# Windowed attention and a gated MLP on one core: 168 keys per 64 queries, four-step scores, split weighing sums, and a new order of all engines

## The chip, the core and the metric

The kernel runs on one core of a Trainium2 chip. The metric is device time in microseconds (us) of one launch, lower is better; runs of the same kernel are compared by their median. A change of less than 0.2% (1.2 us here) can't be told from no change.

Names of the engines, as the profile has them: PE is TensorE's matmuls and PEld its weight loads, DVE is VectorE, ACT ScalarE, POOL GpSimd, SP SyncE, which here only issues DMAs.

## The reference

```python
batch, n_heads, seq, head_dim = (4, 8, 768, 64)
n_global, n_local = (8, 96)

scores = scale * np.matmul(q, k.transpose(0, 1, 3, 2))
keep = (pos[None, :] < n_global) | ((rel >= 0) & (rel < n_local))     # rel = query - key
scores = np.where(keep, scores - slopes * dist, -1e9)
a = np.exp(scores - scores.max(-1, keepdims=True))
a = a / (a.sum(-1, keepdims=True) + 1e-9)
x = np.matmul(a, v)                      # to (3072 tokens, 512)

h = x @ w_in                             # 512 x 2048
g = h * np.tanh(np.log1p(np.exp(h)))
out = g @ w_out                          # 2048 x 512
```

Each query sees the 96 keys up to itself and the first 8 keys of its sequence. All inputs are float32. The kernel computes most products in float16 as three: a number is cut into a high and a low half, and high x high, high x low and low x high are summed in PSUM.

## The kernel before, in words

The 3072 tokens are 12 chunks of 256 (`ci` = 0 to 11; three chunks are one sequence). A chunk has two blocks of 128 queries (`blk`), and attention goes by steps `t`: eight to a chunk, `t = 8*ci + 4*g + 2*blk + a2`, each for one block and one pair of heads. The first block of a sequence sees only its own 128 keys, every other block sees 232: the 96 before it, the 8 global ones, and its own 128. The first three chunks (`CF32`) do attention in float32 with PE transposes. From `ci` = 3 on (the fourth chunk) it is float16 in halves, and these are its steps, with the letters by which the program calls them:

- `s` **scores**: one call does two steps (`a2` = 0, 1), 24 matmuls of 64 rows x 64 columns x 168 moving elements: three products, two heads (upper and lower half of the array), and two halves of 64 queries (`need`, left and right half of the array). Output is in two PSUM banks, `SC`.
- `t` **largest** (DVE): adds the bias mask `mb` and takes the maximum over 232 columns. `y` **exps** (ACT): exponential and sum of the row.
- `g`, `p` **high_a, low_a**: the two float16 halves of the weights, 512 numbers per partition each (232 padded to two blocks of 128, two heads).
- `X` **turn_a**: a DMA transpose of 8 blocks of 128, issued by SP, gives `AT`.
- `W` **weigh**: for each head, 6 matmuls: three products for the 104 far keys (`vc`) and three for the 128 own keys (`vo`). Stationary is `AT`, 128 columns wide; 64 elements move. 12 matmuls a step, 6 in a first block.
- `x` **window_v**: copies the far rows of v to partitions 0 to 103 of `vc`, two DMAs per block. `R`, `T`, `U`, `V` divide by the row sums, cut in halves and turn the result into `xT`.

The MLP of a chunk is eight blocks `m`: `i` **moe_in** (24 matmuls of 256 elements), `j u n r G H z Z` on ACT, DVE and POOL, and `o` **moe_out** (12 matmuls of 512 elements). `Q` and `Y` bring the output out. `k` are checks at the end: a matmul of ones counts bad values (`k1`), and DVE reduces the count to one flag (`k2`), which every engine reads before the program may end.

The weights come as float64 words, and are made into float16 halves by DVE, ACT and POOL (`w A S B C D E`) during about the first 160 us. `e` are matmuls on a constant tile that do nothing but occupy PE.

The order of the whole work is a list written into the program, `PROGRAM`: each engine and each queue takes its own instructions in the order of this list, and never another. Letter and number are the step and its index; a `'` sends a copy or a subtraction to DVE instead of ACT or POOL.

```python
need = [(slice(0, D), slice(0, WN - D)), (slice(D, P), slice(D, WN))]           # scores, not a first block
for kk in range(nk):                                                            # weigh
    for x, y in ((0, 0), (0, 1), (1, 0)):
        nc.tensor.matmul(pav[:, cols], AT[rows_, (x * 2 + j) * nk + kk, :], vs[kk][rows_, y, cols], ...)
```

Of the kernel before, what the change touches and what calls it, by code (L numbers as in the profile page):

```python
# [110 lines left out]
def windowed(st, tc, loc):  # L111
# [14 lines left out]
    OWN = FB  # L126
    STEP = P + NGMAX
# [101 lines left out]
    def window_v(ci):  # L229
        b, c = divmod(ci, NCHB)  # L230
        vc = stk.tile([P, 2, DM], F32, name="vc")
        if ci < CF32:
            far = L.v[b, 0:NGMAX, :]
# [55 lines left out]
    mb0 = cp.tile([P, H, P], BF16, name="mb0")  # L289

# [9 lines left out]
    def units(i):  # L300

        for m in (mb0, mb):
            nc.vector.tensor_scalar(m, m, SQ, None, op0=ALU.mult)

    fills = []

    def begin(n):  # L310

        if not fills:
            fills.append(mt.tile([P, DM], I32, name="ws", bufs=WB).bitcast(F16)[:, 0:DM])
            nc.vector.memset(fills[0], 1.0)
        fill = fills[0]
        bank = ps.tile([P, 2, CH], F32, name="ph").rearrange("p j t -> p (j t)")
        for i in range(n):
            nc.tensor.matmul(bank, fill[:, 0:P], fill, start=True, stop=True)
# [87 lines left out]
    def width(nk):  # L406
        return P if nk == 1 else WN

    def blocks(A, nk):
        if nk == 1:  # L410
            return A[:, :, 0:P].unsqueeze(2)
        return bass.AP(A.tensor, A.offset, [list(A.ap[0]), [W, 2], [FB, 2], [1, P]])

# [4 lines left out]
    def scores(t):  # L418

        ci, g, blk, _, first, nk = shape(t)  # L420
        w = width(nk)
        sc = SC
        col0 = OWN if first else blk * STEP
        rows_ = slice(blk * P, (blk + 1) * P)
        if ci < CF32:
            qr, kr = raw[2 * ci + g]
            terms = ((qr, kr),)
        else:
            (qh, ql), (kh, kl) = split[2 * ci + g, "q"], split[2 * ci + g, "k"]
            terms = ((qh, kh), (ql, kh), (qh, kl))  # L430
        need = [(slice(0, D), slice(0, D)), (slice(D, P), slice(0, P))] if first else [(slice(0, D), slice(0, WN - D)), (slice(D, P), slice(D, WN))]
        for a2 in range(2):
            for n, (x, y) in enumerate(terms):
                for j in range(2):
                    half = slice(j * D, (j + 1) * D)
                    for r, c in need:
                        nc.tensor.matmul(sc[j][r, a2, c], x[half, a2, blk * P + r.start:blk * P + r.stop], y[half, a2, col0 + c.start:col0 + c.stop], start=(n == 0), stop=(n == len(terms) - 1))  # L437
            pend[t + a2] = [x[:, a2] for x in sc]

    def largest(t):  # L440
        ci, g, blk, a2, first, nk = shape(t)
        w = width(nk)
# [5 lines left out]
        for j in range(2):  # L448
            h = g * GH + 2 * a2 + j
            m = mb0[:, h, :] if first else mb[:, h, :]  # L450
# [3 lines left out]
    def exps(t):  # L454
        ci, g, blk, a2, first, nk = shape(t)
        rs, nm = stat[ci, blk]
        A = pend[t][:, :, 0:width(nk)]
# [4 lines left out]
    def halved(t):  # L462
        nk = shape(t)[-1]
        A, hl = pend[t]
        flat = hl.rearrange("p a b w -> p (a b w)")[:, 0:4 * nk * P]
        return blocks(A, nk), flat, flat.rearrange("p (a b k w) -> p a b k w", a=2, b=2, k=nk), nk

    def high_a(t, other=False):
        pend[t] = (pend[t], at.tile([P, 2, 2, W], F16, name="hl", bufs=3))
        A, _, hl, _ = halved(t)  # L470
        copy(hl[:, 0], A, 1.0, other)

    def low_a(t, other=False):
        A, _, hl, _ = halved(t)
        rest(hl[:, 1], A, hl[:, 0], other)

    def turn_a(t):
        _, flat, _, nk = halved(t)
        AT = at.tile([P, 8, P], F16, name="AT", bufs=4)
        nc.sync.dma_start_transpose(AT[:, 0:4 * nk, :], flat)  # L480
# [18 lines left out]
    def weigh(t):  # L499
# [5 lines left out]
        vs = [vown[ci][:, blk]] if nk == 1 else [vcmp[ci][:, blk], vown[ci][:, blk]]  # L505
        if ci < CF32:
            pair = slice((g * GH // 2 + a2) * P, (g * GH // 2 + a2 + 1) * P)
# [5 lines left out]
            return  # L513
        for j in range(2):
            h = g * GH + 2 * a2 + j
            cols = slice(h * D, (h + 1) * D)
            n, last = 0, 3 * nk - 1
            for kk in range(nk):
                rows_ = slice(0, P if kk == nk - 1 else FB)
                for x, y in ((0, 0), (0, 1), (1, 0)):  # L520
                    nc.tensor.matmul(pav[:, cols], AT[rows_, (x * 2 + j) * nk + kk, :], vs[kk][rows_, y, cols], start=(n == 0), stop=(n == last))  # L521
                    n += 1
# [23 lines left out]
    def times_rb(n, other=False):  # L546
# [3 lines left out]
        rbs = at.tile([P, DM], F32, name="rb", bufs=1)  # L550
# [155 lines left out]
    v1 = cp.tile([1, NALL], F32, name="v1")  # L706
# [4 lines left out]
    def checks(i):  # L711
# [36 lines left out]
        e8 I0 x0 q1 v0 K0 K1 M0' M3' L3' L0 L1 L5 M2 L2 s0 e4 t0 t1 f0 M5' y0 L6 M1 y1 L4 s2 P1 P0 t3 F1' y3 t2 w0 q2 e2 P3 q3 x1 w2 v1 F3' L7' y2 F0 s4 W1  # L748
        P2 W0 t5 t4 M7' F2' M4' y5 y4 M6 B0 R0 s6 P4 W3 P5 O0 t6 A0' t7 S0' F4 w1 y6 F5 y7 P6 s8 C0 t8 P7 W5 W4 W2 t9 m0 R1 D0 F6 y8 F7 w3 q4 s10 P8 T0' t10
        t11 B2 A2' U0 y9 O1 P9 s12 W7 W6 w7 w4 w5 x2 q5 v2 w6 t13 y10 m1 F9 F8 y11 P10 W9 P11 W8 t12 S2' F11' B1 T1' C2 y13 F10 y12 E0 s14 W10 P12 W11 P13  # L750
# [213 lines left out]
```

## Time and profile before

| what | us |
|---|---|
| median of 3 runs | 606.42 (605.76 to 606.97) |
| the profiled execution, its own time | 605.27 |
| its span, first to last instruction | 603.4 |
| PE busy, share of the span | 594.3, 98% |
| ACT / DVE / POOL busy | 454.1 / 437.1 / 150.7 |

The first three lines of time differ by what lies around the span (1.87 us) and by the spread of the runs. Busy time is the union of an engine's instructions; since matmuls are pipelined, the time that a matmul costs is better read from one start to the next than from its duration. PE's clock was granted in full over the whole span, but for the first few microseconds.

### The profile page before, as it was taken

The numbers are of one execution on the slowest core, as the hardware profiler recorded it, in microseconds if no ns is written. First come the engines' busy times: TensorE is split into PE (matmuls) and PEld (weight loads), VectorE is DVE, ScalarE is ACT, GpSimd is POOL, SyncE is SP. The second block draws the span as 40 slices with busy tenths as digits, with TensorE's granted clock in tenths as the row PEclk, the third lists the DMA queues.
The fourth block names the chain that finished last, engine by engine and source line by source line (L and its number), as shares of the span: only waits on it lengthen the run. The fifth ranks groups of instructions, "written<-read, shape, count | busy, mean of one in ns | idle before, by whom it ended". The sixth has DMA issues, their size and how long they took to land.

```text
span 603.4 us, 15002 instructions
## 1 busy us (share of the span) xinstructions
PE 594.3 (98%) x5775; PEld 412.3 (68%) x5775; DVE 437.1 (72%) x1188; ACT 454.1 (75%) x1130; POOL 150.7 (25%) x128
## 2 busy tenths in 40 slices
PE   7999999999999999999999999999999999999997
PEld 3678677785567676767666676767667766766784
DVE  7899988998978795693876667675786777462433
ACT  6899999989978777569766778677877864665653
POOL 0033321331040423123134422141242121301020
PEclk9999999999999999999999999999999999999999
DMA  8999664332295481634354443562446241310001
GB/s 207 275 261 337 230 167 132 107 97 64 80 197 110 64 213 32 166 98 113 66 147 113 134 122 92 146 147 55 106 62 150 68 111 44 89 36 0 36 1 39
DMA packets 123387, 71.14 MB, mean 118 GB/s; under 512 B 91792, under 2 KB 113168, under 8 KB 123312
## 3 DMA queue, kind: packets, MB, share of 16 engines
q1 hardware_dynamic: 122736, 69.88, 46.3%
q8 instruction: 46, 0.75, 0.5%
q10 hardware_dynamic: 576, 0.27, 0.3%
q14 instruction: 29, 0.24, 0.1%
HBM read 38.62 MB, written 6.29 MB: 74 GB/s over the span
## 4 chain that ended last, share of the span: by engine, by line
PE 90%; DMA 5%; ACT 2%; SPq 1%; issue 0%; DVE 0%; ACTq 0%; DVEq 0%
PE ph L597 41%; PE po L662 36%; PE pav L662 4%; PE pav L521 4%; PE sc L437 4%; DMA kr<-kd 2%; DMA AT<-hl 2%; DMA vo<-v 2%; PE pav L512 1%; PE ph L490 1%; SPq L480 0%; PE ph L543 0%; ACT A L460 0%; ACT u L623 0%; ACT AT L148 0%
## 5 line engine op out<-in xcount | busy, mean ns | idle before, releaser
L597 PE MATMUL ph<-xT,wts 128*128 128x256 f16 x2304 | 263.5, 273 | 0.0
L597 PEld LDWEIGHTS <-wts 128*128 128x128 f16 x2304 | 223.1, 98 | 34.5 <-issue 0.4
L662 PE MATMUL po<-wts,gt 128*128 128x512 f16 (+1 forms) x1056 | 234.5, 374 | 0.0
L662 PEld LDWEIGHTS <-gt 128*128 128x128 f16 x1248 | 115.7, 98 | 118.1
L615 ACT ACTIVATE e<-ph 128x512 f32<-128x512 f32 x90 | 53.2, 591 | 96.3 <-PE ph L597 96.1
L152 POOL TENSOR_TENSOR gt<-gf,gt 128x512 f16<-128x512 f32 x50 | 61.9, 1240 | 228.8 <-DVE gt L146 154.5
L635 DVE CUSTOM_DVE_ANT_0 gf<-gf,u 128x512 f32<-128x512 f32 x96 | 72.4, 757 | 49.5 <-ACT u L627 47.6
L460 ACT ACTIVATE A<-A,nm 128x232 f32<-128x232 f32 (+1 forms) x192 | 88.2, 461 | 11.9 <-DVE nm L451 11.9
L631 DVE SCALAR_TENSOR_TENSOR gf<-e,ph 128x512 f32<-128x512 f32 x90 | 61.0, 683 | 49.3 <-ACT e L615 48.3
L152 POOL TENSOR_TENSOR hl<-A,hl 128x512 f16<-128x512 f32 (+1 forms) x43 | 50.3, 1179 | 110.6 <-ACT hl L148 43.5
L451 DVE CUSTOM_DVE_ANT_0 A<-sc,mb 128x232 f32<-128x232 f32 (+1 forms) x192 | 63.6, 375 | 12.8 <-PE sc L437 12.7
L627 ACT ACTIVATE u<-u 128x512 f32<-128x512 f32 x96 | 59.7, 625 | 1.9
L619 ACT ACTIVATE u<-e 128x512 f32<-128x512 f32 x96 | 59.8, 624 | 1.7
L623 ACT ACTIVATE u<-u 128x512 f32<-128x512 f32 x96 | 59.7, 623 | 1.6
L152 POOL TENSOR_TENSOR wts<-ws,wts 128x512 f16<-128x512 f32 x18 | 22.7, 1267 | 82.3 <-ACT wts L148 75.6
L152 DVE TENSOR_TENSOR gt<-gf,gt 128x512 f16<-128x512 f32 x46 | 34.3, 748 | 6.9 <-ACT gt L148 6.3
L460 ACT ACTIVATION_READ_ACCUMULATOR A<-A,nm 128x1 f32 x192 | 36.2, 188 | 0.0
L521 PEld LDWEIGHTS <-AT 128*128 128x128 f16 (+1 forms) x792 | 29.3, 97 | 7.6 <-DMA AT<-hl 1.2
L148 ACT ACTIVATE gt<-gf 128x512 f16<-128x512 f32 x39 | 24.3, 623 | 11.3 <-DVE gmax L635 9.2
L662 PE MATMUL pav<-wts,gt 128*128 128x512 f16 (+1 forms) x192 | 28.7, 299 | 0.0
L521 PE MATMUL pav<-vo,AT 128*128 128x64 f16 x432 | 28.0, 192 | 0.0
L146 DVE TENSOR_SCALAR gt<-gf 128x512 f16<-128x512 f32 x57 | 25.7, 453 | 1.5
(130 smaller groups left out, 563.3 us busy)
## 6 DMA issues: line engine op xcount, KB each, us to landing
wts<-w_in SPq DMA_DIRECT2D x12, 512.0 KB
wts<-w_out SPq DMA_DIRECT2D x12, 512.0 KB
qr<-qT SPq DMA_DIRECT2D x23, 256.0 KB
kr<-kd SPq DMA_DIRECT2D x32, 184.0 KB
out<-ob SPq DMA_DIRECT2D x23, 256.0 KB
vr<-v SPq DMA_DIRECT2D x9, 512.0 KB
vc<-vo SPq DMA_DIRECT2D x15, 192.0 KB
wr<-w_in SPq DMA_DIRECT2D x4, 512.0 KB
```

Source lines behind the costliest of these rows:

```text
L152: (nc.vector if other else nc.gpsimd).tensor_tensor(out, in_, high, op=ALU.subtract)
L451: nc.vector.tensor_tensor_reduce(out=A[:, j, 0:w], in0=sc[j][:, 0:w], in1=m, scale=-1.0 / (UNIT if ci < CF32 else UNIT * SQ), scalar=3.0e3 ...
L460: nc.scalar.activation(A[:, j], A[:, j], AF.Exp, bias=nm[:, h:h + 1], scale=-1.0, accum_out=rs[:, h:h + 1])
L521: nc.tensor.matmul(pav[:, cols], AT[rows_, (x * 2 + j) * nk + kk, :], vs[kk][rows_, y, cols], start=(n == 0), stop=(n == last))
L597: nc.tensor.matmul(ph[:, j, :].rearrange("p (b t) -> p b t", b=2), wv4[:, 2 * fb, x, c * P:(c + 1) * P], xT[:, :, y * NCC + c, :], start=( ...
L615: nc.scalar.activation(mish[m]["e"], mish[m]["h"], AF.Exp, scale=-1.0 / (SV * SW), accum_out=esum[:, m:m + 1])
L619: nc.scalar.activation(u, mish[m]["e"], AF.Square, bias=0.5)
L623: nc.scalar.activation(mish[m]["r"], mish[m]["u"], AF.Ln, bias=0.25 / RS, scale=1.0 / RS)
L627: nc.scalar.activation(r, r, AF.Exp, scale=-1.0)
L631: nc.vector.scalar_tensor_tensor(gf, mish[m]["e"], 0.5, mish[m]["h"], op0=ALU.add, op1=ALU.mult)
L635: nc.vector.tensor_tensor_reduce(out=gf, in0=gf, in1=mish[m]["r"], scale=SG / (SV * SW * RS), scalar=0.0, op0=ALU.mult, op1=ALU.max, accum ...
L662: nc.tensor.matmul(pos[ci][t + k][:, cols], gt[:, x, j, t * P:(t + 1) * P], wv4[:, 2 * fb + 1, y, cols], start=(fb == 0 and n == 0), stop= ...
```

## The change

Only chunks from `ci` = 3 on compute otherwise than before:

- Keys are kept per half of 64 queries. A row holds the 168 keys that its half can see (`SEEN` = 104 + 64) instead of 232, so `t` and `y` go over 168 columns and there is a mask `mb2` for it, put together from `mb` by `units`. A first block keeps 128.
- `s` does four steps in one call (two calls a chunk instead of four); only `ci` = 3 keeps two. The second block's scores go to the two `pav` banks, which were for the sums of `W` alone.
- The halves of the weights are 128 columns `main` (key 40 to 167 of the 168) and a block `few`, in which the first 40 keys stand three times side by side: high, low and, for the third product, high again. A transpose has 6 blocks instead of 8.
- `W` does each head as 4 products for each half of 64 queries: three of 128 keys and one of 3 x 40 = 120 rows. That is 16 matmuls a step (12 in a first block) with 64 stationary columns, the two halves side by side in the array; they write to the upper and the lower 64 partitions of `pav`.
- For this `window_v` lays v out anew: per block three larger copies and six of 40 rows, 9 DMAs instead of 2, some of which read what the ones before them have written. For even chunks they go to the buffers `wr` of the weights, which are free by then. Half of the `AT` tiles go to the buffers `hs`.
- `e` uses the broadcast tile of ones (no tile has to be filled first); its calls are 9, 4 and 2 matmuls (before 8, 4, 2). `rb` goes to the buffer of `xhl`, and `v1` to that of `mb`.
- `PROGRAM` is new in all.

```diff
@@ window_v @@
+            src = vo[:, 0] if t else vown[ci - 1][:, 1]
+            far = vo[0:NGMAX, 0] if c == 0 else vcmp[ci - 1][1][P - D - NGMAX:P - D, 0:2]
+            k = P - NPREV + REST
+            nc.sync.dma_start(vb[0:P - k, 0:2], src[k:P])
+            nc.sync.dma_start(vb[P - k:P - D, 0:2], far)
+            nc.sync.dma_start(vb[P - D:P, 0:2], vo[0:D, t])
+            for n, y in enumerate((0, 0, 1)):
+                r = n * REST
+                nc.sync.dma_start(vb[r:r + REST, 2], src[k - REST:k, y])
+                nc.sync.dma_start(vb[r:r + REST, 3], vb[P - D - REST:P - D, y])
@@ scores @@
+            n = 2 if ci == CF32 else 4
+            other = [ps.tile([P, DM], F32, name=f"pav{j}", bufs=1).rearrange("p (a w) -> p a w", a=2) for j in range(2)] if n == 4 else SC
+            for u in range(t, t + n):
+                _, _, blk, a2, first, _ = shape(u)
+                sc = pend[u] = [x[:, a2] for x in (other if blk else SC)]
+                w = width(u)
+                for n, (x, y) in enumerate(((qh, kh), (ql, kh), (qh, kl))):
+                    for j in range(2):
+                        half = slice(j * D, (j + 1) * D)
+                        for r in (0, D):
+                            k = OWN if first else blk * STEP + r
+                            nc.tensor.matmul(sc[j][r:r + D, 0:w], x[half, a2, blk * P + r:blk * P + r + D], y[half, a2, k:k + w], start=(n == 0), stop=(n == 2))
@@ high_a @@
-        copy(hl[:, 0], A, 1.0, other)
+        copy(main[:, 0], A, 1.0, other)
+        if few is not None:
...
+            both = bass.AP(few.tensor, few.offset, [list(few.ap[0]), [P, 2], [2 * REST, 2], [1, k]])
+            copy(both, A[:, :, 0:k].unsqueeze(2).broadcast_to([P, 2, 2, k]), 1.0, other)
@@ weigh @@
-            for kk in range(nk):
-                rows_ = slice(0, P if kk == nk - 1 else FB)
-                for x, y in ((0, 0), (0, 1), (1, 0)):
-                    nc.tensor.matmul(pav[:, cols], AT[rows_, (x * 2 + j) * nk + kk, :], vs[kk][rows_, y, cols], start=(n == 0), stop=(n == last))
+            terms = [(P, j, 0), (P, j, 1), (P, 2 + j, 0)] + ([] if nk == 1 else [(3 * REST, 4 + j, 2)])
+            for n, (k, x, y) in enumerate(terms):
+                for r in range(2):
...
+                    nc.tensor.matmul(pav[r * D:(r + 1) * D, cols], AT[0:k, x, r * D:(r + 1) * D], vs, start=(n == 0), stop=(n == len(terms) - 1))
```

A stretch of the list, the calls that PE gets in chunk 4 (`ci` = 4), before and now, all other letters left out:

```
before  s32 W27 i23 W31 o20 W30 o21 s34 o22 i25 i24 s36 i26 o23 s38 i27 W33 o24 o25 W32 i28 o26 s40 W35 W37 W36 W34 o27
now     s32 o21 o22 i24 s36 i25 i26 o23 i28 o24 i27 W36 W33 W39 W34 W35 W38 W37 W32 i30 o25 o26 s40
```

What moved is that the eight `W` of a chunk now stand in one row, behind both score calls; it is the same in the other eight chunks.

Three places in the order of the engines.

PE, the first weighing of chunk 4, before: `AT` is the turned weight tile, `vc` the far and `vo` the own rows of v, and `pav0` the sum.

```order
L597 MATMUL ph_2920<-xT_2624,wts_96 128x256
L521 LDWEIGHTS AT_2787
L521 MATMUL pav0_2958<-vc_2477,AT_2787 128x64
L521 LDWEIGHTS AT_2787
L521 MATMUL pav0_2958<-vc_2477,AT_2787 128x64
L521 LDWEIGHTS AT_2787
L521 MATMUL pav0_2958<-vc_2477,AT_2787 128x64
L521 LDWEIGHTS AT_2787
L521 MATMUL pav0_2958<-vo_1692,AT_2787 128x64
```

And the first weighing of that chunk now (`hs` is a turned weight tile in its new buffer, `wr` the new layout of v):

```order
L630 MATMUL ph_3120<-xT_2626,wts_97 128x256
L555 LDWEIGHTS hs_2973
L555 MATMUL pav0_3147<-wr_2248,hs_2973 64x64
L555 LDWEIGHTS hs_2973
L555 MATMUL pav0_3147<-vo_1707,hs_2973 64x64
L555 LDWEIGHTS hs_2973
L555 MATMUL pav0_3147<-wr_2248,hs_2973 64x64
L555 LDWEIGHTS hs_2973
L555 MATMUL pav0_3147<-vo_1707,hs_2973 64x64
```

Each full-width matmul has become two of 64 stationary columns, one for each half of the queries; 128 of them now follow one another in a chunk.

SP, the copies of v for chunk 5 (lines 248 and 249) between the transposes (L480 of the weights, L580 of `xT`), before:

```order
L480 DMA_TRANSPOSE AT<-hl 128x8x128
L580 DMA_TRANSPOSE xT<-xhl 128x8x128
L248 DMA vc<-vo 96x1024
L249 DMA vc<-vc 8x1024
L248 DMA vc<-vo 96x1024
L249 DMA vc<-vc 8x1024
L480 DMA_TRANSPOSE AT<-hl 128x8x128
```

And now, the first of the two blocks of that chunk (lines 259 to 265), behind the last transpose of chunk 4's weights:

```order
L508 DMA_TRANSPOSE hs<-hl 128x6x128
L259 DMA vc<-vo 56x1024
L260 DMA vc<-wr 8x1024
L261 DMA vc<-vo 64x1024
L264 DMA vc<-vo 40x512
L265 DMA vc<-vc 40x512
L264 DMA vc<-vo 40x512
L265 DMA vc<-vc 40x512
L264 DMA vc<-vo 40x512
L265 DMA vc<-vc 40x512
L259 DMA vc<-vo 56x1024
```

Four DMAs have become eighteen, and both transposes of `xT` now wait behind them.

DVE at the end of the program, before (`v` and `done_i` are the reduction of the checks, `ob` a piece of the output):

```order
L725 TENSOR_SCALAR v_108<-sc_102 1x142
L726 TENSOR_REDUCE v_110<-v_108 1x1
L727 TENSOR_REDUCE v_109<-sc_102 1x12
L728 TENSOR_REDUCE v_110<-v_109 1x1
L729 TENSOR_REDUCE v_110<-sc_102 1x1
L730 TENSOR_TENSOR v_110<-v_110 1x1
L731 TENSOR_SCALAR v_110<-v_110 1x1
L732 SCALAR_TENSOR_TENSOR done_i<-v_110,fl 1x1
L146 TENSOR_SCALAR ob<-pav_8509 128x128
```

And now:

```order
L148 TENSOR_SCALAR ob<-pav_9120 128x128
L758 TENSOR_SCALAR mb<-sc_103 1x142
L759 TENSOR_REDUCE v_110<-mb 1x1
L760 TENSOR_REDUCE v_109<-sc_103 1x12
L761 TENSOR_REDUCE v_110<-v_109 1x1
L762 TENSOR_REDUCE v_110<-sc_103 1x1
L763 TENSOR_TENSOR v_110<-v_110 1x1
L764 TENSOR_SCALAR v_110<-v_110 1x1
L765 SCALAR_TENSOR_TENSOR done_i<-v_110,fl 1x1
```

The reduction has moved behind the last piece of the output, and on PE the matmul that feeds it behind the last `o` (before it stood in front of that).

## Rows read from the trace of the kernel before

**Rows 1.** The page's first part: busy us, share of the span, instructions.

```profile
PE 594.3 (98%) x5775; PEld 412.3 (68%) x5775; DVE 437.1 (72%) x1188; ACT 454.1 (75%) x1130; POOL 150.7 (25%) x128
```

**Rows 2.** Busy time of each engine in five stretches (us from the start).

```profile
core 0: us, PE busy (x) PEld busy (x) DVE busy (x) ACT busy (x) POOL busy (x), PEclk, DMA share, GB/s
0.00:31.20 31.20, 27.20 (x302) 16.80 (x303) 24.80 (x112) 23.38 (x80) 1.95 (x8) 1.00 0.96 241
31.20:60.70 29.50, 29.29 (x350) 22.95 (x348) 28.33 (x95) 28.95 (x80) 10.68 (x9) 1.00 1.03 302
60.70:165.00 104.30, 104.30 (x828) 71.06 (x827) 96.14 (x214) 97.94 (x214) 26.52 (x21) 1.00 0.43 123
165.00:560.00 395.00, 394.53 (x3956) 271.88 (x3954) 270.21 (x723) 283.30 (x716) 105.76 (x87) 1.00 0.45 103
560.00:603.40 43.40, 38.96 (x347) 29.61 (x344) 17.62 (x47) 20.50 (x43) 5.76 (x5) 1.00 0.07 26
```

**Rows 3.** Groups by line and form: busy us, mean ns, idle before.

```profile
L521 PE MATMUL pav<-vo,AT 128*128 128x64 f16 x432 | 28.0, 192 | 0.0
...
L521 PE MATMUL pav<-vc,AT 104*128 104x64 f16 x360 | 24.8, 192 | 0.5 <-DMA AT<-hl 0.4
```

**Rows 4.** Timeline of PE, 300 to 312 us: start, length, instructions merged.

```profile
303.26 2.78 PE L597 MATMUL ph<-xT,wts 128*128 128x256 f16 x24
305.98 0.63 PE L437 MATMUL sc<-wc,ws 64*64 64x168 f16 x24
306.54 2.79 PE L597 MATMUL ph<-xT,wts 128*128 128x256 f16 x24
309.17 0.25 PE L521 MATMUL pav<-vc,AT 104*128 104x64 f16 x3
...
309.80 0.25 PE L521 MATMUL pav<-vo,AT 128*128 128x64 f16 x3
309.88 2.32 PE L662 MATMUL po<-wts,gt 128*128 128x512 f16 x10
```

**Rows 5.** One score call, timeline cut off at 306.06, 306.11 and 306.18 us.

```profile
305.98 0.27 PE L437 MATMUL sc<-wc,ws 64*64 64x168 f16 x4
...
305.98 0.34 PE L437 MATMUL sc<-wc,ws 64*64 64x168 f16 x8
...
305.98 0.41 PE L437 MATMUL sc<-wc,ws 64*64 64x168 f16 x12
```

**Rows 6.** Timeline of PE, 21 to 23.4 us: a float32 step of 64-column matmuls.

```profile
21.10 0.66 PE L490 MATMUL po<-idn,A 128*128 128x128 f32 x4
21.68 1.09 PE L543 MATMUL ph<-idn,ri 128*64 128x128 f32 x16
22.70 0.66 PE L490 MATMUL po<-idn,A 128*128 128x128 f32 x4
```

**Rows 7.** Groups by form: the maxima and the exponentials.

```profile
L460 ACT ACTIVATE A<-A,nm 128x232 f32<-128x232 f32 x160 | 75.8, 476 | 9.8 <-DVE nm L451 9.8
...
L451 DVE CUSTOM_DVE_ANT_0 A<-sc,mb 128x232 f32<-128x232 f32 x160 | 56.0, 392 | 9.6 <-PE sc L437 9.5
...
L460 ACT ACTIVATE A<-A,nm 128x128 f32<-128x128 f32 x32 | 12.4, 388 | 2.0 <-DVE nm L451 2.0
...
L451 DVE CUSTOM_DVE_ANT_0 A<-sc,mb 128x128 f32<-128x128 f32 x32 | 7.6, 286 | 3.2 <-PE sc L437 3.2
```

**Rows 8.** The chain that ended last: two early loads, one wait for a transpose.

```profile
7.74 9.19 DMA kr<-kd
16.94 9.34 DMA vo<-v
...
384.57 4.27 DMA AT<-hl
```

**Rows 9.** Timeline of SP, 300 to 312 us: issues of one transpose and two copies.

```profile
302.32 0.60 SPq L248 DMA_DIRECT2D vc<-vo  x1
...
302.97 0.73 SPq L249 DMA_DIRECT2D vc<-vc  x1
...
305.19 1.27 SPq L480 DMA_TRANSPOSE AT<-hl  x1
```

**Rows 10.** Timeline of the end: the checks on DVE, and PE's last matmuls.

```profile
594.94 0.29 DVE L725 TENSOR_SCALAR v<-sc 1x142 f32<-1x142 f32 x1 [0.96 <-PE sc L722]
...
596.37 0.21 DVE L732 SCALAR_TENSOR_TENSOR done_i<-v,fl 1x1 int32<-1x1 f32 x1
...
598.12 0.83 PE L662 MATMUL pav<-wts,gt 128*128 128x128 f16 x12
```

More of the change, by code (lines that the diff above doesn't have):

```diff
@@ L126, in windowed @@
     OWN = FB
+    SEEN = FB + D
+    REST = SEEN - P
     STEP = P + NGMAX
@@ L298, in mask_far, with units @@
         masked(mb[:, h, :], rel, h, other)
[L300 to L308, printed above, removed]
+    def units(i, other=False):
+        if i == 0:
+            copy(mb0, mb0, SQ, not other)
+        else:
+            half = slice(0, D) if i == 1 else slice(D, P)
+            copy(mb2[half], mb[half, :, 0:SEEN] if i == 1 else mb[half, :, D:], SQ, not other)
     def begin(n):
[L312 to L315, printed above, removed]
         bank = ps.tile([P, 2, CH], F32, name="ph").rearrange("p j t -> p (j t)")
         for i in range(n):
-            nc.tensor.matmul(bank, fill[:, 0:P], fill, start=True, stop=True)
+            nc.tensor.matmul(bank, ones.broadcast_to([P, P]), ones.broadcast_to([P, DM]), start=True, stop=True)
     NPC = 2 * NFB
@@ L404, in shape, with width @@
         return ci, g, blk, a2, first, 1 if first else 2
[L406 to L412, printed above, removed]
+    def width(t):
+        nk = shape(t)[-1]
+        return P if nk == 1 else WN if where(t)[0] < CF32 else SEEN
     SC = [ps.tile([P, 2, W], F32, name=f"sc{j}", bufs=1) for j in range(2)]
@@ L420, in scores @@
         ci, g, blk, _, first, nk = shape(t)
-        w = width(nk)
+        if ci >= CF32:
+            (qh, ql), (kh, kl) = split[2 * ci + g, "q"], split[2 * ci + g, "k"]
+            n = 2 if ci == CF32 else 4
[10 more added lines that the diff above has]
+                            nc.tensor.matmul(sc[j][r:r + D, 0:w], x[half, a2, blk * P + r:blk * P + r + D], y[half, a2, k:k + w], start=(n == 0), stop=(n == 2))
+            return
         sc = SC
         col0 = OWN if first else blk * STEP
[L424 to L430, printed above, removed]
+        qr, kr = raw[2 * ci + g]
         need = [(slice(0, D), slice(0, D)), (slice(D, P), slice(0, P))] if first else [(slice(0, D), slice(0, WN - D)), (slice(D, P), slice(D, WN))]
         for a2 in range(2):
[L433 to L437, printed above, removed]
+            for j in range(2):
+                half = slice(j * D, (j + 1) * D)
+                for r, c in need:
+                    nc.tensor.matmul(sc[j][r, a2, c], qr[half, a2, blk * P + r.start:blk * P + r.stop], kr[half, a2, col0 + c.start:col0 + c.stop], start=True, stop=True)
             pend[t + a2] = [x[:, a2] for x in sc]
@@ L441, in largest @@
         ci, g, blk, a2, first, nk = shape(t)
-        w = width(nk)
+        w = width(t)
         sc = pend[t]
@@ L456, in exps @@
         rs, nm = stat[ci, blk]
-        A = pend[t][:, :, 0:width(nk)]
+        A = pend[t][:, :, 0:width(t)]
         for j in range(2):
```

174 lines of the change are left out of this document (97 added, 77 removed).

## The prediction
> **What bounds the kernel now.** I read the page's busy shares first: PE is at 98%, and no other engine is above 75% [rows 1]. A share over the whole span can hide stages, so the second view is the busy time in five stretches [rows 2]. From 31 to 560 us PE is idle for 0.68 us in all; its idle time lies ahead of that (4.0 us, the first loads) and behind it (4.4 us, the end of the program). DVE and ACT are above 90% until 165 us, while the weights are split, and at 68% and 72% after. So the time is the sum of PE's work, plus a start and an end, as long as the others keep up. An edit is worth what it takes off PE; what it takes off DVE and ACT is worth nothing behind 165 us.
>
> A busy PE says little of what one matmul costs, so I use starts in its timeline. A weighing matmul is listed with 192 ns [rows 3], but 24 of them take from 309.17 to 309.88 us: 0.71 us, 29.6 ns each [rows 4]. A score call takes from 305.98 to 306.54 us, 0.56 us for 24 matmuls [rows 4]. Cut off at three times, it shows 4, 8 and 12 matmuls begun, four more each 0.07 us [rows 5]: the four quarters of the array run side by side, and a set of four costs what 168 elements cost. Six sets are 0.43 us, so 0.13 us of the call is something else. The block ahead of it, 24 matmuls of 256 elements, takes 2.72 us to the score call and 2.63 us where a weighing follows [rows 4]: another 0.1 us. A stay in quarters thus costs 0.23 us beside its work.
>
> **The change, part by part.**
>
> *Scores.* The matmuls and their elements stay: 12 per step, sets of four. (In a first block one of each pair grows from 64 to 128 elements, but its partner was 128 already, so the set's time stays.) Chunks 4 to 11 had four calls and have two: 16 stays fewer, 16 x 0.23 = 3.7 us off PE.
>
> *Weighing sums, before.* 60 steps of 12 and 12 steps of 6 are the 792 matmuls of rows 3; at 29.6 ns, 23.4 us. They come and go without a change of mode.
>
> *Weighing sums, now.* 60 steps of 16 and 12 of 12 are 1104 matmuls of 64 columns, 552 pairs, one of each pair for either half of the array. What a pair costs the trace does not show in float16. Upper bound: one after the other at today's pace, 59 ns. Lower bound: the 64 moving elements alone, by the 0.109 us that 256 elements take [rows 4], 27 ns. The nearest row is the float32 step with 64 columns by 128 rows: 16 matmuls of 128 elements in 1.02 us, 64 ns each, where 4 of the same elements at full width take 0.58 us before it, 145 ns each [rows 6]. Pairs do overlap there. Weight loads of 64 columns keep up with sets of 72 ns [rows 5]; whether they do at 30 ns is open. I take 29.6 ns a pair, today's pace with two columns' worth of work under it: 552 x 29.6 = 16.3 us. Nine stays of this mode, one per chunk, cost 9 x 0.23 = 2.1 us. Sum 18.4, which is 5.0 us less than 23.4.
>
> The Trainium skill speaks against this edit: its page TensorEngine Tiling (Array Packing), section Performance Considerations, gives each matmul about 60 cycles of overhead, so that one of few elements costs no less than one of 60. At 2.4 GHz that would be an estimated 25 ns a matmul, 27.6 us for 1104; by that page the sum would rise by 11.3 us, and the kernel would be slower than before. The trace does not bear it out as a price per matmul where tiles run side by side: four matmuls begin in 0.07 us, 18 ns each, with 168 elements [rows 5].
>
> *Narrower maxima and exponentials.* 120 of each go from 232 to 168 columns. Between the rows for 232 and 128 columns [rows 7] a maximum goes from 392 to 327 ns and an exponential from 476 to 422 ns: 7.8 us of DVE, 6.5 us of ACT. High and low halves become two instructions each with fewer elements, about even. I cost this at nothing: PE covers both engines from 165 us on [rows 2]. If PE ceased to bound, up to some 7 us would come back as gain.
>
> *Copies of v.* SP issues 18 DMAs per later chunk instead of 4, at 0.60 to 0.73 us each [rows 9]: some 12 us, and two waits for copies that read earlier copies. Of a chunk's 50 us SP also needs 8 transposes of 1.27 us [rows 9]. Behind the copies of chunk 5 stand the two transposes of `xT` of chunk 4. By the new list PE has seven blocks `i` or `o` (2.6 us each) and two score calls between the weighing of chunk 4 and its first `i`, 20 us. I cost the copies at nothing; the thinnest cover is the last chunk, where three blocks, 8.1 us, must hide `R`, `T`, `U` and a transpose, which was waited for up to 4.27 us [rows 8].
>
> *Weighing in one row.* All eight transposes of a chunk must have landed when its row begins; before, each `W` had a place of its own. In chunk 4 six blocks (16 us) and the score call lie between the second call and the row. ACT and DVE, busy for 72% and 68% of such a time [rows 2], have some 12 us of work in it, and the last step needs a transpose of up to 4.27 us [rows 8] behind that. It fits with little left. For nine rows, and for score calls that wait until DVE has emptied four banks, I take 1.0 us of new waits in all (bounds 0 and 4).
>
> *Start.* The list now loads the first weights and v (128 x 1024 numbers of 4 bytes each, 0.5 MB) ahead of the second group's queries and keys, where 0.2 MB of far rows stood. At 241 GB/s [rows 2] the 0.8 MB more are 3.5 us. Loads are on the chain there [rows 8]. Against it, PE has 4.0 us of idle time until 31 us, all of it with a reason in the first loads, so little can be won. I take +0.7 us (bounds -1 and +2).
>
> *End.* The checks took from 594.94 to 596.58 us, hidden behind PE, which ended at 598.95 [rows 10]. Now their matmul and DVE's part, 1.64 us, begin when PE is through and a last piece is copied, and every engine reads the flag before it ends. The output's landing covers some of the 4.4 us behind PE. I take +0.8 us (bounds 0 and +1.6).
>
> **Sum**, against the profiled execution's own 605.27 us: -3.7 - 5.0 + 1.0 + 0.7 + 0.8 = -6.2, so 599.1 us. The median of the runs is 1.15 us above that execution, so I give **600.2 us** for a median. With every open price at its good end (27 ns a pair, start -1, no waits, no tail) it is 595.3; with pairs at 29.6 and the others at their bad ends, 605.3.
>
> **Rivals.**
>
> *A matmul keeps a price of its own, however narrow it is (slower).* Either the two halves do not run side by side, or PE can't issue so fast. The place is the nine rows of `W`: 128 matmuls and 128 loads follow each other, and the forecast needs four of these per 29.6 ns, 7.4 ns each. If each matmul still takes 29.6 ns, the sums cost 32.7 + 2.1 us, 16.4 more than forecast: 616.6 us. It decides from 41 ns a pair on, where the forecast's 6.2 us are used up. For it: a row of 256 such instructions occurs nowhere in the trace, and a score call's eight per 0.07 us [rows 5] are 9 ns each and only 48 in a row. Against it: these same sets, and the float32 pairs [rows 6]. Chance 0.13. The Trainium skill's 60 cycles, from the section named above, are this rival at a milder price.
>
> *New waits eat the gain.* PE waits about 1 us ahead of each of nine rows of `W`, or the first 60 us, where DVE and ACT have no slack [rows 2], lose several us by the new order: 605 to 609 us. For it: all engines were reordered, and SP carries three times the copies. Against it: behind 165 us the other engines have a quarter of their time to spare. Chance 0.17. Half of this is about even with before.
>
> *Forecast*, 0.70.
>
> **How the numbers follow.** A median can be told from no change from 0.2% on, 1.2 us. Faster: the forecast's 0.70, and 0.02 from the waits that eat only part. Within 0.2% (605.2 to 607.6): 0.12, mostly waits. Slower: 0.16, a matmul's own price and the worse part of the waits. The range goes from 596, near the good end, to 608, which takes in the forecast's bad end and half of the waits. Outside are about 0.15 above and 0.05 below.
>
> **What would show it.** Right: in the profile after, PE stays above 98%, a row of eight weighings takes 1.9 to 2.2 us from its first start to the next block, a four-step score call 1.0 us, and ACT and DVE fall by 5 to 8 us in all with no effect. The time behind PE's last matmul grows from 4.4 to about 5 us. Wrong: a row of `W` of 3 us and more (the first rival), or idle time of PE ahead of `W`, `s` or `i` that names a DMA, ACT or DVE (the second); or a start that reaches the first `i` later than 31.2 us by more than 2 us.

## The result, and the profile after

| | before | after |
|---|---|---|
| median of the runs, us | 606.09 (604.65 to 606.97, 4 runs) | 599.02 (598.45 to 599.12, 4 runs) |
| ratio after to before, 95% interval | | 0.9884 [0.9863, 0.9904] |
| profiled execution, own time | 605.27 | 598.95 |
| its span | 603.4 | 597.2 |

The kernel is 1.2% faster. The forecast was 600.2 us, within 596 to 608. The profiled execution came out at 598.95 us, where the sum said 599.1.

The first part of the page of after, to be read against [rows 1]:

```profile
PE 586.9 (98%) x6088; PEld 407.6 (68%) x6088; DVE 435.9 (73%) x1265; ACT 438.5 (73%) x1138; POOL 146.6 (25%) x163
```

ACT has lost 15.6 us of work and DVE 1.2 us. PE's busy share is the same, and its sum has fallen by 7.4 us, while it has 313 more matmuls in the records.

The windows of after, cut where the stages end, with the columns of [rows 2]:

```profile
0.00:31.45 31.45, 27.64 (x296) 17.61 (x297) 26.95 (x121) 22.99 (x80) 3.74 (x10) 1.00 0.96 252
31.45:60.30 28.85, 28.85 (x359) 23.49 (x356) 27.98 (x90) 27.16 (x75) 8.34 (x7) 1.00 0.98 303
60.30:165.00 104.70, 104.70 (x821) 72.07 (x820) 98.66 (x224) 96.07 (x212) 26.59 (x22) 1.00 0.51 143
165.00:553.10 388.10, 386.69 (x4274) 264.76 (x4272) 264.10 (x783) 271.74 (x733) 103.82 (x122) 1.00 0.45 100
553.10:597.20 44.10, 39.03 (x347) 29.71 (x345) 18.17 (x49) 20.59 (x43) 4.08 (x3) 0.97 0.07 26
```

The first two stretches hold the same float32 work as in before; they end at 60.30 us, where before needed 60.7. From there to 553 us PE is idle for 1.41 us. From the end of the float32 attention to the start of the last MLP matmul it was 538.0 us before and is 531.4 now (531.4 also in a second profile of this kernel, *same_again* below). So the time went out of PE's work in the later chunks. There the timeline of PE in after shows a score call, and a row of weighing (start, length, instructions merged):

```profile
302.44 5.34 PE L695 MATMUL po<-wts,gt 128*128 128x512 f16 x24
307.71 0.63 PE L440 MATMUL sc<-wc,ws 64*64 64x168 f16 x24
308.17 0.61 PE L440 MATMUL pav<-wc,ws 64*64 64x168 f16 x24
308.71 3.56 PE L630 MATMUL ph<-xT,wts 128*128 128x256 f16 x31
...
329.65 0.22 PE L555 MATMUL pav<-vc,hs 128*64 128x64 f16 x1
329.65 0.22 PE L555 MATMUL pav<-vo,hs 128*64 128x64 f16 x1
...
331.80 0.39 PE L630 MATMUL ph<-xT,wts 128*128 128x256 f16 x2
```

The four-step call takes 1.00 us to the next block, and 0.09 us more is lost at its entry: 1.09 us. A two-step call cost 0.562 us and the same 0.094 at its entry, 0.656 us; twice that is 1.31, so a stay that is saved gives 0.22 us. The row of 128 products starts its pairs together, and takes 2.15 us to the next block, 2.24 with its entry. From pair to pair it is 31.7 ns on average.

Summed over all PE starts behind the float32 attention, the attention groups, with the gaps at their entries, fell from 47.44 to 40.68 us (-6.8). The MLP's own blocks rose by 0.4 us of small gaps, and the checks' matmul (0.2 us) went behind the last MLP matmul. Together that is the 6.6 us between 538.0 and 531.4. The waits of PE in after (us in total, times, longest):

```profile
PE sc L450 <- DVE nm L464: 1.4, 2, 0.9
PE pav L555 <- DMA hs<-hl: 1.3, 1, 1.3
PE ph L328 <- DVE ones L143: 1.0, 1, 1.0
PE pav L540 <- ACT AT L150: 0.9, 2, 0.5
```

Two of them are new: a row of weighing at 283 us waits for the last of four transposes, and two score calls of the start wait for the maxima. SP had waited 3.8 us for a low copy of DVE there, and then issued the last three transposes one behind the other, at 279.3, 280.6 and 281.9 us; the last landed at 284.4 us. The end of after, last matmuls and DVE's part of the checks [rows 10]:

```profile
591.10 0.83 PE L695 MATMUL pav<-wts,gt 128*128 128x128 f16 x12
...
591.87 0.26 PE L755 MATMUL sc<-ind,ones 128*1 128x240 f16 x1
592.17 0.29 DVE L758 TENSOR_SCALAR mb<-sc 1x142 f32<-1x142 f32 x1 [0.24 <-PE sc L755]
...
593.59 0.21 DVE L765 SCALAR_TENSOR_TENSOR done_i<-v,fl 1x1 int32<-1x1 f32 x1
```

DVE's 1.63 us now begin behind PE's last matmul, the checks' own. From the start of the last MLP matmul (591.72) to the end of the span it is 5.45 us, where it was 4.65.

### The profile page after: what moved, and what is told of

Read it like the earlier page. It is cut to its first block, busy times and chain, and to the rows that moved or that the text cites. A ratio compares the mean times of both kernels' runs of the same rounds, so it can differ in the third digit from the quotient of the medians.

```text
span 597.2 us, 15925 instructions
## 1 busy us (share of the span) xinstructions
PE 586.9 (98%) x6088; PEld 407.6 (68%) x6088; DVE 435.9 (73%) x1265; ACT 438.5 (73%) x1138; POOL 146.6 (25%) x163
## 4 chain that ended last, share of the span: by engine, by line
PE 83%; ACT 5%; DMA 4%; DVE 3%; SPq 3%; issue 2%; POOL 0%; ACTq 0%; DVEq 0%; POOLq 0%
PE ph L630 37%; PE po L695 32%; PE pav L695 4%; PE pav L555 3%; DMA kr<-kd 2%; ACT A L473 2%; PE pav L540 2%; PE sc L440 1%; PE sc L450 1%; PE pav L440 1%; PE po L518 1%; PE ph L576 1%; PE ph L518 1%; SPq L265 1%; ACT e L648 1%
## 5 line engine op out<-in xcount | busy, mean ns | idle before, releaser
L695 PEld LDWEIGHTS <-gt 128*128 128x128 f16 x1248 | 117.5, 98 | 120.4 <-DVE gt L154 0.3
L154 POOL TENSOR_TENSOR gt<-gf,gt 128x512 f16<-128x512 f32 x49 | 59.9, 1225 | 210.9 <-DVE gt L148 117.3
L473 ACT ACTIVATE A<-A,nm 128x168 f32<-128x168 f32 (+2 forms) x192 | 82.0, 429 | 28.7 <-DVE nm L464 28.5
L668 DVE CUSTOM_DVE_ANT_0 gf<-gf,u 128x512 f32<-128x512 f32 x96 | 69.1, 722 | 41.6 <-ACT u L660 39.3
L154 POOL TENSOR_TENSOR hl<-A,hl 128x80 f16<-128x80 f32 (+1 forms) x79 | 46.8, 615 | 143.0 <-DVE hl L148 65.3
L464 DVE CUSTOM_DVE_ANT_0 A<-sc,mb 128x168 f32<-128x168 f32 (+2 forms) x128 | 37.7, 337 | 5.6 <-PE sc L440 4.3
L154 POOL TENSOR_TENSOR wts<-ws,wts 128x512 f16<-128x512 f32 x16 | 20.4, 1280 | 72.7 <-ACT wts L150 34.9
L148 DVE TENSOR_SCALAR hl<-A 128x256 f16<-128x256 f32 (+1 forms) x66 | 20.7, 352 | 12.9 <-ACT A L473 7.7
L150 ACT ACTIVATE hl<-A 128x256 f16<-128x256 f32 (+1 forms) x66 | 22.3, 381 | 5.3 <-issue 4.5
```

Of the source, the lines that this page charges most:

```text
L148: nc.vector.tensor_scalar(out, in_, scale, None, op0=ALU.mult)
L150: nc.scalar.activation(out, in_, AF.Copy, scale=scale)
L154: (nc.vector if other else nc.gpsimd).tensor_tensor(out, in_, high, op=ALU.subtract)
L473: nc.scalar.activation(A[:, j], A[:, j], AF.Exp, bias=nm[:, h:h + 1], scale=-1.0, accum_out=rs[:, h:h + 1])
L668: nc.vector.tensor_tensor_reduce(out=gf, in0=gf, in1=mish[m]["r"], scale=SG / (SV * SW * RS), scalar=0.0, op0=ALU.mult, op1=ALU.max, accum ...
L695: nc.tensor.matmul(pos[ci][t + k][:, cols], gt[:, x, j, t * P:(t + 1) * P], wv4[:, 2 * fb + 1, y, cols], start=(fb == 0 and n == 0), stop= ...
```

## The experiments

Three sets of four kernels ran, each set on one chip with its own runs of the kernel before: medians 604.32 (set 1), 604.86 (set 2) and 605.04 us (set 3). Ratios below are to these. Set 3 has the changed kernel without an edit too (*same_again*, 598.74 us). Set 1 is compared with half_by_half (599.13 us), which came out at the changed kernel's time; set 2 has no such run, and its times stand beside 598.74 and 599.02 us of other chips.

### Do the halves of the array work side by side?

*half_by_half* (set 1): each half's products of one head in a row.

```diff
-            for n, (k, x, y) in enumerate(terms):
-                for r in range(2):
+            for r in range(2):
+                for n, (k, x, y) in enumerate(terms):
```

> The same 552 pairs, products and order of engines as the changed kernel, but each half's four products are issued one after another, so that neighbours on PE use the same half of the array. Theory (the weighing is paid by the pair, because the two halves work side by side): a row of 128 products goes from 2.24 us to 3.9 to 4.1 us, nine such rows, and the kernel to about 614 us. Rival (PE issues one product after another at a pace of its own, and the halves never overlapped): rows stay at 2.2 to 2.3 us and the time at 599 us, within 1 us.

Measured: 599.13 us (598.02 to 600.04), ratio 0.9912 [0.9881, 0.9943]; the rows of 128 still take 2.17 us to the next block. The rival's number came. Taken alone this run would say that the halves do not matter. But the timeline of the same row, in this kernel, shows the two streams of loads begin as before:

```profile
329.28 0.22 PE L555 MATMUL pav<-vc,hs 128*64 128x64 f16 x1
329.29 0.22 PE L555 MATMUL pav<-vo,hs 128*64 128x64 f16 x1
```

A product that reads `vc` is one of the first half, one that reads `vo` here one of the second. (A fourth, of 120 rows, reads `vc` on either half.) In the program four of the first half now stand ahead of the second's, yet a `vo` starts some 10 ns behind the first `vc`. So products that stand four places down the order had already begun, and the test had been too weak. The next one puts dozens in a row.

*half_rows* (set 3): the products of a stretch are held until its division (`rows`), then all of one half are issued, then all of the other.

```diff
+    def by_halves():
+        for r in range(2):
+            for pav, cols, j, nk, vo, vb, AT in held:
...
     def rows(n):
+        by_halves()
```

> Each stretch of weighing up to its division is issued by halves: all products of one half of the array, some 40 to 80 in a row, then all of the other; products and pairs stay the same in number. Theory (the two halves work side by side, and four products in a row were hidden because PE holds several products ready for each half): now one half stands idle, a row of 128 goes from 2.24 us to 3.8 to 4.0 us, and the time rises by 13 to 16 us to about 613 us. Rival (PE issues at 16 ns a product whichever half it goes to): rows of 2.24 us and no change, within 1 us.

Measured: 612.05 us (611.75 to 612.62), ratio 1.0123 [1.0103, 1.0143], 13.3 us above the run without an edit in this set. The timeline of a row of 128:

```profile
334.18 0.44 PE L560 MATMUL pav<-vc,hs 128*64 128x64 f16 x8
334.45 0.92 PE L560 MATMUL pav<-vc,AT 128*64 128x64 f16 x24
335.21 0.57 PE L560 MATMUL pav<-vc,hs 128*64 128x64 f16 x13
...
338.06 0.50 PE L637 MATMUL ph<-xT,wts 128*128 128x256 f16 x3
```

It takes 3.88 us to the next block in place of 2.15. The 24 products of one half take from 334.45 to 335.21 us, 31.7 ns each, which is what a pair costs in the changed kernel. This is the theory's size: the pair is the unit that is paid, and the gain of the split sums stands or falls with neighbours on different halves. It also explains half_by_half: a few products ahead are enough to fill the other half.

### What does a stay in quarters cost?

*two_step_calls* (set 1).

```diff
-            n = 2 if ci == CF32 else 4
-            for u in range(t, t + n):
+            for u in range(t, t + 2):
...
-  s36 q12 p33' g32
+  s36 i25 s38 q12 p33' g32
```

> The scores of the later chunks are computed by two steps a call again, the second call one PE block behind the first in 15 of 16 places; all else stays as in the changed kernel. Theory (each separate stay in the quadrant form costs PE 0.2 us beside its 72 ns rounds): 15 more stays, +3.3 us, so about 602.3 us, and score calls of 0.65 us in the trace in place of 1.09 us. Rival (the gain of the scores came from the new order, the stays cost nothing): 599 us within 0.5 us.

Measured: 614.58 us (613.22 to 615.88), ratio 1.0172 [1.0144, 1.02]. This is 15.5 us above half_by_half of the same set, not 3.3. The timeline of PE shows a pair of the split calls, and the waits show the rest:

```profile
312.68 0.63 PE L439 MATMUL sc<-wc,ws 64*64 64x168 f16 x24
313.24 2.79 PE L629 MATMUL ph<-xT,wts 128*128 128x256 f16 x24
315.97 0.63 PE L439 MATMUL pav<-wc,ws 64*64 64x168 f16 x24
```

```profile
PE ph L629 <- DVE gf L663: 8.3, 7, 2.1
PE po L694 <- DVE gt L148: 1.6, 1, 1.6
```

Each call costs 0.56 us again, so the price of the stays is as forecast: 15 x 0.22 = 3.3 us. The profiled spans differ by 14.5 us (611.4 against 596.9); the other 11 us are waits of PE for DVE (8.3 + 1.6 in these rows, and a new one of 1.3 for `nm`). The second call comes one block (2.6 us) later, and DVE waits for it with the maxima: ten waits, 22.1 us, of a kind that half_by_half does not have. What stands behind the maxima in DVE's order, the MLP's gate (`gf`, `gt`), is late for PE. The total is therefore no measure of the stays; the rows are. It is a measure of how little the order bears: 2.6 us on 15 calls cost 11.

### Is the relief of DVE and ACT free?

*give_back* (set 1) and *act_back* (set 3).

```diff
# give_back
+        if ci >= CF32 and t % 4 == 1:
+            nc.vector.tensor_tensor_reduce(out=A[:, j, 0:w], ...)
...
+        if t % 4 == 1:
+            copy(main[:, 0], A, 1.0)
# act_back
+        if t % 2 == 1:
+            copy(main[:, 0], A, 1.0)
```

> Work is given back to DVE and ACT: in every fourth step of the later chunks both maxima are computed twice (36 more on DVE, about 14.7 us of busy time) and the main values' high copy is made twice (18 more on ACT, about 7 us). Theory (what the change took off DVE and ACT was off the path that sets the end, since PE is busy 98% of the span): 599.0 us, at most 0.7 us more by one or two new waits. Rival (part of the gain came from the relief of DVE and ACT): +2 us or more, with PE waits for DVE of 2 us or more in the later chunks.

> ACT alone gets work back: in every second step of the later chunks the main values' high copy is made twice, 36 more of about 0.4 us, 14.4 us in all, about what the change took off ACT (454.1 to 438.5 us). Theory (ACT's relief was worth nothing, and the 3.7 us that the other run lost came from DVE): up to 0.7 us slower than the run without an edit. Rival (ACT's relief was part of the gain): 2 us slower or more, with PE waits for tiles that ACT's copies stand ahead of.

Measured: give_back 602.69 us (601.81 to 605.78), ratio 0.9971 [0.9955, 0.9987], 3.6 us above half_by_half; act_back 605.09 us (603.92 to 608.46), ratio 0.9997 [0.9985, 1.0009], 6.35 us above the run without an edit. The theory fell both times. In give_back the added work was less than expected, 5.9 us of DVE's busy time (442.0 against 436.1) and 6.9 of ACT's. The windows of 165 to 250 us, first after, then act_back:

```profile
165.00:250.00 85.00, 84.86 (x951) 57.54 (x949) 62.24 (x193) 66.38 (x179) 26.68 (x32) 1.00 0.54 120
```

```profile
165.00:250.00 85.00, 82.45 (x929) 55.17 (x928) 63.71 (x194) 68.00 (x185) 22.72 (x27) 1.00 0.54 119
```

PE stands idle for 2.55 us in place of 0.14, with ACT busy for 80% of the stretch in place of 78%. (The profiled execution of act_back, 608.46 us, was the slowest of its thirteen: its granted clock was 0.50 from 15.9 to 22.7 us, and it ends the float32 attention 3.9 us later than same_again. From there to the last MLP matmul it takes 537.7 us against 531.4, which is the 6.3 us of the medians.) One such wait of act_back, from the timelines of DVE and PE:

```profile
198.92 0.58 DVE L154 TENSOR_TENSOR hl<-A,hl 128x256 f16<-128x256 f32 x2 [1.38 <-ACT hl L150]
...
200.49 0.68 DVE L666 SCALAR_TENSOR_TENSOR gf<-e,ph 128x512 f32<-128x512 f32 x1
...
201.22 2.02 PE L632 MATMUL ph<-xT,wts 128*128 128x256 f16 x17 [1.32 <-DVE gf L666]
```

ACT's high copy comes late, DVE waits 1.38 us for it with the low copy, the gate's operations stand behind that, and PE waits 1.32 us for `gf`. So 13.2 us more on ACT (451.6 against 438.4 us busy) cost 6.35 us, though ACT is idle for a quarter of the span. That is shown for work added to this order. What the 15.6 us that the change took off ACT were worth in the old order was not tried; there PE's gaps in the MLP were 0.7 us in all, so not much was to be had.

### The end

*checks_early* (set 1): `o94 k1 Z95' o95 k2 Q11` in place of `o94 Z95' o95 k1 Q11 k2`.

> The last instructions of the checks stand ahead of the last votes again, as in the kernel before; nothing else moves. Theory (the checks' last reduction on DVE stands on the path to the end in the changed kernel): the stretch from the last matmul's start to the span's end goes from 5.30 back to 4.65 us, and the time falls by 0.65 us to 598.4 us. Rival (the stretch is set by the waiting for the output's last write, not by DVE): 5.30 us and 599.0 us stay.

Measured: 598.11 us (597.25 to 598.5), ratio 0.9892 [0.987, 0.9915]; 1.0 us below half_by_half, which is less than the medians can tell apart. The rows show it:

```profile
589.68 0.21 DVE L765 SCALAR_TENSOR_TENSOR done_i<-v,fl 1x1 int32<-1x1 f32 x1
...
591.43 0.83 PE L695 MATMUL pav<-wts,gt 128*128 128x128 f16 x12
```

DVE's last check now starts at 589.68 us, ahead of PE's last matmul, an MLP one that starts at 592.05 us. From the start of the last MLP matmul to the end it is 4.49 us in place of 5.45 (5.30 from the check's matmul, which was the last before). The theory holds for this stretch.

### The start

*flags_late* (set 2): `f0` behind `Q2`. *real_fill* (set 2):

```diff
-            nc.tensor.matmul(bank, ones.broadcast_to([P, P]), ones.broadcast_to([P, DM]), start=True, stop=True)
+            nc.tensor.matmul(bank, fill[:, 0:P], fill, start=True, stop=True)
```

> The seven flag operations f0 on DVE (1.4 us) stand behind the transposes of the first chunk's second head group (Q2 in the order) in place of ahead of the masks; nothing else moves. Theory (PE's first two score calls wait for DVE, and DVE is late by the flags and by the first ramp): the PE wait for the maxima's tile near the start goes from 1.4 us to under 0.5 us, and the time falls by 0.8 to 1.4 us. Rival (PE is still at its lower clock in that stretch and the keys' loads come last): the wait changes its name to a DMA, and the time stays within 0.4 us of the changed kernel.

> PE's first products read a filled tile, as in the kernel before, in place of the column of ones read again and again; the new order stays. Theory (the granted clock rises later in the changed kernel, 6.0 us after the first product in place of 3.3 us, because those first products read one repeated column): full clock at 5 to 6 us of the span, and the time falls by up to 1 us. Rival (the clock rises by something else, and the fill on DVE delays the first product to 2.7 us): no gain, or up to 0.5 us slower.

PE's first rows in after, in flags_late and in real_fill:

```profile
1.02 4.02 PE L328 MATMUL ph<-ones 128*128 128x512 f16 x9 [1.02 <-DVE ones L143]
...
8.68 0.57 PE L450 MATMUL sc<-kr,qr 64*64 64x168 f32 x6 [0.88 <-DVE nm L464]
```

```profile
5.92 0.65 PE L450 MATMUL sc<-kr,qr 64*64 64x64 f32 x12 [0.26 <-DMA kr<-kd]
6.51 1.05 PE L328 MATMUL ph<-ones 128*128 128x512 f16 x4
7.54 1.00 PE L450 MATMUL sc<-kr,qr 64*64 64x168 f32 x16
```

```profile
4.35 4.02 PE L334 MATMUL ph<-ws 128*128 128x512 f16 x9 [4.35 <-DVE n_neg L731]
```

flags_late: the wait for the maxima is gone, the second score call starts at 7.54 in place of 8.68 us, the first MLP block at 29.74 in place of 31.45 us, and the profiled span is 595.8 us, of the fastest of five runs. The median, 598.9 us (597.54 to 600.08), ratio 0.9909 [0.9896, 0.9922], does not show it: the five runs spread over 2.5 us. Unclear as a whole, shown for the wait.

real_fill: 600.03 us (599.28 to 600.47), ratio 0.9917 [0.9904, 0.993]. The theory fell. The fill stands behind other operations on DVE, so PE's first product starts at 4.35 us, and the first MLP block at 32.84 us. The first products run 0.427 us apart, which is 512 columns at 1.2 GHz (the profile's clock column says 1.00 there all the same). They are still 0.40 to 0.43 us apart up to 10.19 us, 5.8 us behind the first. In after the pace of 0.22 us is first seen at 7.2 us, 6.2 us behind the first, in flags_late at 6.5 us, and in same_again, which is after without an edit, at 6.2 us. In this profile reading a filled tile did not bring 2.4 GHz sooner; what does was not found, and two executions of one kernel differ by 1 us.

### The wait at 283 us

*w52_last* (set 2): `W53 W52 R12 T12' U12` behind `W55`.

> In the row of weighing of chunk 6's first half the two steps that wait for SP's last transposed load stand at the row's end, with the row's rest behind them; nothing else moves. Theory (one transposed load comes 1.27 us late there, and later steps have theirs): the wait for hs at 283 us goes, the row takes 2.0 us in place of 3.4 us, and the time falls by 1.0 to 1.3 us. Rival (the next work on PE was to wait for DVE or ACT anyway): the wait moves to the next MLP blocks and the time stays within 0.4 us.

Measured: 601.02 us (600.26 to 601.37), ratio 0.9931 [0.9918, 0.9944]; 2 us above the changed kernel in other sets. PE's timeline in after, then in w52_last with the windows around it:

```profile
284.41 0.57 PE L555 MATMUL pav<-vo,hs 128*64 128x64 f16 x24 [1.27 <-DMA hs<-hl]
...
285.67 2.79 PE L630 MATMUL ph<-xT,wts 128*128 128x256 f16 x24
288.30 2.75 PE L695 MATMUL po<-wts,gt 128*128 128x512 f16 x12
```

```profile
285.89 0.38 PE L555 MATMUL pav<-vo,hs 128*64 128x64 f16 x12 [1.96 <-DMA hs<-hl]
286.20 4.46 PE L630 MATMUL ph<-xT,wts 128*128 128x256 f16 x24
290.49 1.67 PE L695 MATMUL po<-wts,gt 128*128 128x512 f16 x7
```

```profile
285.00:288.00 3.00, 2.11 (x24) 1.68 (x25) 1.34 (x3) 2.22 (x5) 0.00 (x0) 0.82 0.33 86
288.00:292.00 4.00, 4.00 (x21) 2.41 (x20) 3.68 (x11) 0.69 (x2) 2.50 (x2) 0.71 0.20 69
```

Both theories missed. The wait became longer, 1.96 us: SP issued the transpose at 281.8 us as before, 15 of its 16 parts landed by 284.33, the last at 285.84 us. Why that one was late stays open. Behind the wait the granted clock, the third number from the end, is 0.82 and 0.71 in these windows. The products of 256 elements stand 0.109 us apart up to 286.9 us, then 0.213 us (1.2 GHz) up to 290.2 us, then 0.109 again; the block of 24 takes 4.30 us where the same block in after, at 1.00, takes 2.63. So 0.85 us in the row and 1.7 us by the clock were lost.

### Taken together

*all_four* (set 2) joins these four edits; *both* (set 3) joins checks_early and flags_late; *same_again* (set 3) is the changed kernel, unedited.

> The checks ahead of the last votes, the flags late, the filled tile and the two steps at their row's end, all in the order of the changed kernel. If the theories of these four hold one by one, their gains add up: 0.65 + 1.1 + 0.5 + 1.2 = about 3.4 us less than the changed kernel, so about 595.6 us (span 593.8 us). If the start is bound by the loads and the wait at 283 us moves on, only the checks are left: about 598.4 us.

> The changed kernel once more, with no edit, on the chip on which the next three run: it is what they are compared with. Every theory expects the time of the changed kernel, 599.0 us within 0.7 us, and a span of 597 us.

> Two edits together that the earlier runs spoke for: the checks' last instructions ahead of the last votes, and the flag operations behind the first chunk's second load of transposes. Theory (two stretches at opposite ends, each on the path): 0.65 us at the end and 1.0 to 1.4 us at the start, so 1.6 to 2.1 us less than the run without an edit on the same chip. Rival (what the start gains is lost to later waits): 0.7 us less.

Measured: all_four 601.85 us (600.45 to 603.94), ratio 0.9947 [0.9928, 0.9966]. The expected sum counted gains that real_fill and w52_last did not have on their own: against some 599 us they stand at +1 and +2 us, and all_four at +3. Its profile shows where w52_last's edit leads when the transpose is not late:

```profile
PE pav L446 <- DVE xmax L574: 2.2, 1, 2.2
PE pav L561 <- DMA hs<-hl: 0.3, 1, 0.3
```

The wait of the row has gone to 0.3 us, and the next score call, at 292 us, waits 2.2 us for the division (`xmax`) that the same edit put at the row's end; its scores go to the `pav` bank that the division reads. So the wait moved on, as the rival of w52_last had it, to another place and at a larger price. same_again 598.74 us (598.2 to 599.19), ratio 0.9902 [0.9883, 0.9922]. both 598.32 us (597.14 to 601.59), ratio 0.9898 [0.9874, 0.9922]: not to be told from same_again. Its profiled execution, of 599.95 us, is one of the two with the lowest mean clock, and the windows show why it is longer:

```profile
13.00:15.00 2.00, 2.00 (x20) 1.34 (x20) 2.00 (x11) 1.86 (x9) 0.18 (x1) 0.50 1.11 225
15.00:17.00 2.00, 1.53 (x11) 0.60 (x7) 0.91 (x7) 1.35 (x4) 0.00 (x0) 0.50 1.11 254
17.00:19.00 2.00, 2.00 (x18) 1.67 (x18) 1.97 (x11) 1.38 (x7) 0.00 (x0) 0.50 1.09 261
```

The granted clock is 0.50 from 13 to 19 us (1.2 GHz), and the first MLP block comes at 32.56 us. Two of six runs had a mean clock of 0.993 (599.95 and 601.59 us); the other four lie at 597.14 to 598.86. The steadiest of these versions is checks_early (597.25 to 598.5 us); by the ratios it can't be told from the changed kernel.

## Why the prediction was right

| step | forecast | measured, profiled execution |
|---|---|---|
| scores | -3.7 | -3.5 (16 x 0.22) |
| weighing sums | -5.0 | -4.2 (23.6 to 19.4, waits left out) |
| new waits | +1.0 | +1.4 (0.4 in the MLP, 1.0 in the attention groups) |
| start | +0.7 | -0.4 |
| end | +0.8 | +0.6 (0.8, less 0.2 of the checks' matmul, which stood ahead of it) |
| sum | -6.2 | -6.1 of a fall of 6.2 |

*Scores.* Right, and shown: the call at 307.71 us, and two_step_calls in its rows.

*Weighing.* The mechanism was right: half_rows shows that the pair is paid. The size was off: "I take 29.6 ns a pair" measured 31.7, 552 x 2.1 ns = 1.2 us. The stay of 0.23 us was 0.21 to 0.22.

*A matmul keeps a price of its own.* This rival is out: a pair costs 31.7 ns in the rows, and it decided from 41 on. Without the other half it is true: half_rows pays 31.7 ns a product, and the kernel is slower than before. The Trainium skill (TensorEngine Tiling (Array Packing), Performance Considerations) gives each matmul about 60 cycles of overhead, an estimated 25 ns at 2.4 GHz; the 31.7 ns of a single half don't speak against that, the 17 ns a product of both halves (2.15 us for 128) do.

*Start.* The step "I take +0.7 us" came out with the other sign, -0.4 us by the end of the float32 attention. The larger loads did not decide: PE's waits until 31 us are 3.8 us as before, of which 2.6 name DVE, 0.9 ACT and 0.3 a load. Seven profiles with this start and no fall of the clock in it (after, same_again, half_by_half, half_rows, w52_last, give_back, two_step_calls) reach that point at 59.6 to 60.4 us. The kernel before has one profile, 60.7, so how far its own start moves is not known, and the sign stays unsettled.

*End.* Right, and shown by checks_early in its rows.

*New waits.* The sum was right within its bounds, the place partly: "All eight transposes of a chunk must have landed when its row begins" was the reason for the one long wait, in one row of nine, but "the thinnest cover is the last chunk" was not where it came. The copies of v, costed at nothing, are named by no wait of PE.

*Narrower maxima and exponentials.* The times that were read off between two widths came true: 326 ns a maximum and 423 ns an exponential of 168 columns, where 327 and 422 were worked out. The sign "ACT and DVE fall by 5 to 8 us in all" failed: ACT fell by 15.6 us and DVE by 1.2, because the new list also moved copies from ACT to DVE.

*Costed at nothing.* "What it takes off DVE and ACT is worth nothing behind 165 us" did no harm to the sum, because the change takes work off them. As a reason it failed: act_back and give_back show that the cover by PE is much thinner than the busy shares of [rows 2] say, 6.35 us for 13.2. The rival of new waits was nearer than it looked: a like amount on ACT would have brought its 605 us.

The total was closer than its terms, and that is luck: weighing and start were off by about 1 us each, with opposite signs.

## What to carry to other kernels

When an operation is split over halves of the array, price the pair, and order neighbours so that they go to different halves; a test that puts only a few products of one half in a row does not tell, since the next ones are already begun. An engine with a quarter of idle time is not a free place. In an order written by hand, follow what stands behind the operation on its queue before costing it at nothing. When a wait is removed by a move in the order, look for it again at the next place that needs what was moved. A gain of a microsecond in the first 30 us can't be read from one profile.

## What the runs showed of the hardware

- Products on one half of the array: 31.7 ns each, 24 in a row; with both halves at work 31.7 ns a pair. Four products in a row on one half cost nothing, dozens cost the full price.
- Products start out of the program's order across the two halves: in half_by_half the other half's first product, fifth in the program, started at 329.29 us, ahead of the next one of the first half at 329.33 us.
- Coming to a form of the array with narrower tiles and leaving it cost 0.21 to 0.22 us a stay, for four quarters (1.31 against 1.09 us) and for two halves (2.24 us for 64 pairs of 31.7 ns).
- A wait of PE of 1.96 us at 284 us (w52_last) and one of 2.2 us at 292 us (all_four) were each followed by a stretch at 1.2 GHz, with products of 256 elements 0.213 us apart. A wait of 1.27 us at 283 us (after) and one of 1.92 us at 413 us (two_step_calls) were followed by a granted clock of 1.00. That the wait causes the fall is not shown.
- The granted clock was 0.50 from 13 to 19 us in one execution of *both*, behind a start in which PE was busy for 10.8 of 13 us; in same_again, busy for 9.9 of 13 us, it stayed at 1.00. At paces of 1.2 GHz near 5 us the clock column said 1.00, so it does not show the clock's first rise.
